# First-layer products of batches 0 and 1 as pairs of 128x64 column halves

## The chip, the cores and the metric

The kernel runs on one core of a Trainium2 chip. The metric is the device time of one execution in microseconds (us); lower is better. Inputs and outputs lie in the chip's memory. One core has a matrix engine (TensorE, PE in the profile, its weight loads listed apart as PEld), VectorE (DVE), ScalarE (ACT), GpSimd (POOL), SyncE (SP), and 16 DMA engines. Sums of products form in PSUM, everything else lies in SBUF.

## The reference, cut to what matters

An attention whose softmax has one more term in the denominator, followed by a two-layer network with a squared ReLU. There are 8 batches, 12 heads, 448 positions, 64 features a head; 3584 tokens, a model width of 768 and a hidden width of 2048.

```python
scale = 1.0 / np.sqrt(q.shape[-1])
scores = scale * np.matmul(q, k.transpose(0, 1, 3, 2))
m = np.max(scores, axis=-1, keepdims=True)
e = np.exp(scores - m)
attn = e / (np.sum(e, axis=-1, keepdims=True) + np.exp(-m) + 1e-09)
x = np.matmul(attn, v)      # then heads side by side: 3584 x 768
...
h = x @ w_in                # 768 x 2048: the first layer
r = np.maximum(h, 0.0)
out = (r * r) @ w_out       # 2048 x 768: the second layer
```

## The kernel before

**Staging.** All eight batches go through the same chain of steps on one core. Scores of a quad of heads (`quad_scores`, tile `sp` in PSUM, products of 64x64 blocks of the array) become exponentials on ACT (`quad_exp`, tiles `et` and `nn`). DVE adds them up (`add_quad`, tile `half`), TensorE sums and multiplies them with v (`sums_of_quad`, `values_step`), ACT forms the reciprocals (`rcp`), and DVE writes the attention's result, transposed, to the batch's tile `xt` (six chunks of 128 features by 448 tokens). Batch 0 is done in two halves of 224 positions at the start (`half_scores` and so on), so that work can begin early.

**The first layer**, which the change touches. For a block of 128 hidden units, `f0`, six products are summed in a PSUM tile `mp`, one for each chunk `dc` of 128 model features: the weights are a 128x128 block of `win`, the moving operand is 448 columns of `xt` (`later_in`, line 513). For a part of batch 0 it is done for two blocks `f0` at once and for 224 columns (`half_in`, line 530), in six pieces of 12 products. All of them go through `product` (line 490), which has two forms. With `cols` false, one matrix product uses the whole 128x128 array. With `cols` true, it is two products of 128 rows by 64 columns, each with half of the weights' columns and the same moving operand; they write partitions 0 to 63 and 64 to 127 of the PSUM tile. In the profile these shapes are 128\*128 and 128\*64. Line 93 is the helper `mm` that records nearly all products, so tiles and shapes tell them apart: `mp<-xt,win` is the first layer, `mp<-wout,gs` the second.

Then ReLU on DVE or ACT (`relu`, tile `rt`), the square on DVE into `gs`, and the second layer in 64x64 blocks (`out_piece`), whose two partial sums DVE adds before the result is stored.

**Who uses which form.** Three stretches of code follow each other. `ORDER` is a list, written out by hand, of steps for the start: batch 0 and most of batches 1 to 3, and in it the first layers of batches 0 and 1 (letters `i` and `j`). `CYCLE` is such a list for a period of two batches; it runs twice, and each run computes 32 first-layer blocks of two earlier batches. The tail computes the first layers of the last two batches (`tile_in`) and the last outputs in order. Before the change the periods alone pass `cols` as true; `ORDER` and the tail leave the default, false:

```python
def later_in(b, f0, c0, c1, cols=False):                             # line 513
"j": lambda n, c0=0, c1=DCH: later_in(*of_tile(n), c0, c1),          # ORDER, line 656
"j": lambda n, c0, c1: later_in(*block(n), c0, c1, True),            # CYCLE, line 741
later_in(b, f0, c, c + 2)                                            # tail, line 783
```

Engines take their instructions in the order of these lists; waits between engines follow from the data. In `ORDER`, the first-layer products stand in blocks between scores, transposes (`transpose_one`, line 207) and values; in the periods they stand in one block.

Of the kernel before, what the change touches and what calls it, by code (L numbers as in the profile page):

```python
# [16 lines left out]
def kernel(  # L17
# [68 lines left out]
    def mp_tile(dtype=FP32):  # L86
        return ring[-1].tile([128, 512 if dtype == FP32 else 1024], dtype, name="mp")
# [4 lines left out]
    def mm(out_, lhsT, rhs, start, stop):  # L92
        return nc.tensor.matmul(out_, lhsT, rhs, start=start, stop=stop)  # L93
# [3 lines left out]
    def load_v_quads(b, g0=0, g1=NQ):  # L97
        if b not in vns:
            vns[b] = v_pool.tile([128, 2, NQ, KC, D], FP16, name="vn")
        vn = vns[b]  # L100
        if b in ON_PE:
            if g1 - g0 == NQ:
                nc.gpsimd.dma_start(out=vn.rearrange("p j g c d -> p (j g) (c d)"), in_=by_pairs["v"][b])
            else:
                nc.gpsimd.dma_start(out=vn[:, :, g0].rearrange("p j c d -> p j (c d)"), in_=by_pairs["v"][b, :, g0::NQ])
            return
        for i in range(2):
            rows_ = vn[64 * i:64 * i + 64].rearrange("p j g c d -> p (j g) (c d)")
            for c0, c1 in ((0, KC - 1), (KC - 1, KC)):
                src = v[:, :, 64 * c0:64 * c1].rearrange("b (hp i) (p t) d -> b i p hp (t d)", i=2, t=c1 - c0)  # L110
                nc.gpsimd.dma_start(out=rows_[:, :, c0 * D:c1 * D], in_=src[b, i])
# [32 lines left out]
    def stage(b):  # L144
        for n, t in (("q", q), ("k", k)):
            st = nc.dram_tensor(f"stage_{n}{b}", (TOTAL,), FP16, kind="Internal").ap()
            stages[n, b] = st
            src = t.rearrange("b h s d -> (b h s d)")
            lo = b * HSD - FRONT
            hi = min(lo + TOTAL, B * HSD)  # L150
            m = (hi - lo) // 1024 * 1024
            for x, y in ((lo, lo + m), (lo + m, hi)):
                if y > x:
                    w = min(y - x, 1024)
                    nc.gpsimd.dma_start(out=st[x - lo:y - lo].rearrange("(r w) -> r w", w=w),
                                        in_=src[x:y].rearrange("(r w) -> r w", w=w), max_dma_last_dim=8192)
            if hi < lo + TOTAL:
                nc.gpsimd.dma_start(out=st[hi - lo:TOTAL].rearrange("(r w) -> r w", r=1),
                                    in_=src[0:lo + TOTAL - hi].rearrange("(r w) -> r w", r=1))
# [3 lines left out]
    def transposed_load(b, i):  # L163
        qk = qk_of(b)
        n, x, c = PLANES[i]
        nc.sync.dma_start(
            out=qk[:, i, 0:c],
            in_=stages[n, b][x:x + c * 2 * D].rearrange("(r c) -> r c", c=2 * D),
            transpose=True,
        )  # L170
# [7 lines left out]
    def tail_keys(b, planes=(1, 2)):  # L178

        if b not in kms:  # L180
            kms[b] = flat.tile([128, H, 64], FP16, name="flatq")
        km = kms[b]
        for which in planes:
            for r in range(2):
                rows_ = slice(64 * r, 64 * r + 64)
                odd, x = (r, 0) if which == 1 else (1 - r, 1 - r)
                src = qks[b][rows_, which, x:x + H * S // 2].rearrange("p (h x) -> p h x", h=H)
                nc.gpsimd.tensor_copy(km[rows_].rearrange("p h (x o) -> p h x o", o=2)[:, :, :, odd],  # L188
                                      src[:, :, S // 2 - 32:S // 2])
# [210 lines left out]
    def quad_scores(m, c):  # L400

        b, g = QUADS[m]
        qk = qks[b]
        if (m, c // 4) not in eqs:
            if g == NQ - 1 and b > 1:
                eqs[m, c // 4] = nat.tile([128, RUN * 2 * S], FP16, name=f"nn{c // 4}")
            else:
                eqs[m, c // 4] = e_pool.tile([128, RUN * 2 * S], FP16, name="et")
        sp = sps["quad", m, c] = s_psum.tile([128, 2, 512], FP32, name="sp")
        if b in ON_PE:  # L410
            for i in range(2):
                for j in range(2):
                    r = slice(64 * j, 64 * j + 64)
                    x = (2 * g + i) * S
                    mm(sp[64 * i:64 * i + 64, j, 0:S], qk[r, 1, x + 64 * c:x + 64 * c + 64],
                       qk[r, 0, x:x + S], start=True, stop=True)
        else:
            n = S // 2
            for j in range(2):
                for i in range(2):  # L420
                    for o in range(2):
                        r = slice(64 * o, 64 * o + 64)
                        h = 2 * NQ * j + 2 * g + i
                        if c == KC - 1:
                            keys = kms[b][r, h, :]
                        else:
                            which, x = (1, h * n + c // 2) if c % 2 == o else (2, h * n + c // 2 + c % 2)
                            keys = qk[r, which, x:x + 190:3]
                        mm(sp[64 * i:64 * i + 64, o, j * n:(j + 1) * n], keys,
                           qk[r, 0, h * n:(h + 1) * n], start=True, stop=True)  # L430

    def quad_exp(m, c):
        exp(chunk_quad(m, c).rearrange("p (o x) -> p o x", o=2), sps.pop(("quad", m, c))[:, :, 0:S])
# [26 lines left out]
    def quad_z(m):  # L460
        zp = zps.pop(m)
        rcp = zqs[m] = z_pool.tile([128, 2, S], FP32, name="rcp")
        nc.scalar.activation(out=rcp, in_=zp[:, :, 0:S], func=AF.Ln, bias=one_b)  # L463
# [23 lines left out]
            nc.vector.tensor_mul(xts[b][:, 2 * g + i, :], xqs[m][i][:, 0:S], zqs[m][:, i, :])  # L487
        del eqs[m, 0], eqs[m, 1], xqs[m], zqs[m]

    def product(out_, lhsT, rhs, start, stop, cols=False):  # L490

        if cols:
            for x in (0, 64):
                mm(out_[x:x + 64], lhsT[:, x:x + 64], rhs, start=start, stop=stop)
        else:
            mm(out_, lhsT, rhs, start=start, stop=stop)
# [13 lines left out]

    hps = {}

    def later_in(b, f0, c0, c1, cols=False):
        if c0 == 0:
            hps[b, "all", f0] = mp_tile()
        hp, xt = hps[b, "all", f0], xts[b]
        for dc in range(c0, c1):
            product(hp[:, 0:S], win[:, dc, f0 * 128:(f0 + 1) * 128], xt[:, dc, :],
                    start=(dc == 0), stop=(dc == DCH - 1), cols=cols)
# [192 lines left out]
    def period(b):  # L712
        m = NQ * (b - 1)
        first = EARLY + 2 * KC * (b - FIRST_PERIOD) // 2

        def following(n):
            ahead, what = ((1, n) if n < 6 else (2, 6) if n < 7 else (1, 6) if n < 8 else (2, n - 8))
            t = b + ahead
            if t < B and (n != 7 or b > FIRST_PERIOD):
                if what < 3:  # L720
                    transposed_load(t, what)
                elif what < 5:
                    tail_keys(t, (what - 2,))
                elif what == 5:
                    load_v_quads(t)
                else:
                    stage(t)

        def block(n):
            return b - 2 + n // NFFB, n % NFFB  # L730

        return {
            "s": lambda x, c: quad_scores(m + x, c),
            "e": lambda x, c: quad_exp(m + x, c),
            "a": lambda x, step: add_quad(m + x, step),
            "S": lambda x: sums_of_quad(m + x),
            "Z": lambda x: quad_z(m + x),
            "M": lambda x: quad_reciprocal(m + x),
            "v": lambda x, c: values_step(m + x, c),
            "X": lambda x: quad_x(m + x),  # L740
            "j": lambda n, c0, c1: later_in(*block(n), c0, c1, True),
            "k": lambda n, act: later_relu(*block(n), act),
            "l": lambda n: later_squared(*block(n)),
            "o": lambda n, f0, f1: out_piece(128 * ((first + n) // 2), HALF * ((first + n) % 2), HALF, range(f0, f1), True),
            "O": lambda n, act: out_first(128 * ((first + n) // 2), HALF * ((first + n) % 2), HALF, act),
            "Q": lambda n: out_second(128 * ((first + n) // 2), HALF * ((first + n) % 2), HALF),
            "d": lambda n: following(n),
        }
# [31 lines left out]

    def tile_in(b, f0):
        for c in range(0, DCH, 2):
            later_in(b, f0, c, c + 2)
        later_relu(b, f0, False)
        later_squared(b, f0)

# [39 lines left out]
```

## Time and profile before

| | |
|---|---|
| median of 3 runs | 392.37 us (391.68 to 394.08) |
| profiled execution | 392.36 us, span from first to last instruction 390.6 us |
| granted TensorE clock | 1.00 in all slices |
| TensorE busy | 381.8 us, 98% of the span, 6432 products |
| DVE, ACT, POOL busy | 65%, 58%, 16% |
| first-layer products | 768 of 128\*64 by 448 columns; 348 of 128\*128 by 448; 72 of 128\*128 by 224 |
| chain that ended last | PE 89%, ACT 5%, the rest 6% |

The busy time counts a stretch in which any product is in flight, and the mean of a product is its latency in the pipeline. As products overlap, the pace of a group must be taken from the starts of its instructions, or from the length of a block in the timeline divided by its products. A line of the timeline gives the start, the length to the end of the last instruction, engine, line, operation, tiles, shape and how many were merged.

### The profile page before, as it was taken

The numbers are of one execution on the slowest core, as the hardware profiler recorded it, in microseconds if no ns is written. First come the engines' busy times: TensorE is split into PE (matmuls) and PEld (weight loads), VectorE is DVE, ScalarE is ACT, GpSimd is POOL, SyncE is SP. The second block draws the span as 40 slices with busy tenths as digits, with TensorE's granted clock in tenths as the row PEclk, the third lists the DMA queues.
The fourth block names the chain that finished last, engine by engine and source line by source line (L and its number), as shares of the span: only waits on it lengthen the run. The fifth ranks groups of instructions, "written<-read, shape, count | busy, mean of one in ns | idle before, by whom it ended". The sixth has DMA issues, their size and how long they took to land.

```text
span 390.6 us, 14257 instructions
## 1 busy us (share of the span) xinstructions
PE 381.8 (98%) x6432; PEld 254.3 (65%) x6432; DVE 253.5 (65%) x468; ACT 228.3 (58%) x308; POOL 61.9 (16%) x96
## 2 busy tenths in 40 slices
PE   9689999999999999999999999999999999999997
PEld 5566656565689865567777665567777755556665
DVE  3887995765765766556968757575878788880000
ACT  5999998586689611249989731248988720001221
POOL 8443420025000700410001240210000000000000
PEclk9999999999999999999999999999999999999999
DMA  8999999999939899903129697901112200001132
GB/s 144 204 204 205 201 199 206 159 203 176 215 84 166 168 186 118 201 2 66 44 59 196 148 178 156 165 4 44 60 48 64 64 23 2 0 0 62 61 82 81
DMA packets 75052, 45.34 MB, mean 116 GB/s; under 512 B 47472, under 2 KB 72944, under 8 KB 74992
## 3 DMA queue, kind: packets, MB, share of 16 engines
q0 software_dynamic: 24752, 22.62, 37.6%
q1 hardware_dynamic: 49952, 21.59, 28.6%
q8 instruction: 50, 0.82, 1.0%
q10 hardware_dynamic: 288, 0.23, 0.2%
q14 instruction: 10, 0.08, 0.1%
HBM read 45.69 MB, written 17.93 MB: 163 GB/s over the span
## 4 chain that ended last, share of the span: by engine, by line
PE 89%; ACT 5%; DMA 2%; DVE 2%; POOL 1%; issue 1%; POOLq 0%; DVEq 0%; ACTq 0%
PE mp L93 79%; PE sp L93 8%; ACT et L254 3%; DMA nn<-in_k_dram 2%; PE mp L207 1%; POOL nn L117 1%; ACT rcp L372 1%; ACT rcp L365 0%; DVE half L441 0%; DVE xt L487 0%; DVE half L443 0%; DVE half L445 0%; ACT rcp L466 0%; ACT rcp L463 0%; DVE half L447 0%
## 5 line engine op out<-in xcount | busy, mean ns | idle before, releaser
L93 PE MATMUL mp<-wout,gs 64*64 64x384 f16 (+2 forms) x2928 | 165.4, 322 | 0.0
L93 PE MATMUL mp<-xt,win 128*64 128x448 f16 (+2 forms) x1188 | 148.3, 347 | 0.1
L93 PEld LDWEIGHTS <-gs 64*64 64x64 f16 (+1 forms) x2928 | 103.8, 106 | 33.9
L93 PEld LDWEIGHTS <-win 128*64 128x64 f16 (+1 forms) x1188 | 83.2, 106 | 63.5 <-issue 4.2
L254 ACT ACTIVATE et<-sp 128x896 f16<-128x896 f32 (+2 forms) x131 | 110.6, 891 | 12.7 <-PE sp L93 12.2
L505 DVE TENSOR_SCALAR rt<-mp 128x448 f16<-128x448 f32 x87 | 54.0, 622 | 15.9 <-PE mp L93 12.9
L509 DVE TENSOR_TENSOR gs<-rt 128x448 f16<-128x448 f16 x128 | 49.4, 404 | 21.9 <-ACT rt L503 20.0
L503 ACT ACTIVATE rt<-mp 128x448 f16<-128x448 f32 x41 | 21.8, 543 | 64.9 <-PE mp L93 50.9
L575 ACT ACTIVATE ot<-mp 128x384 f32<-128x384 f32 (+2 forms) x31 | 14.9, 480 | 70.5 <-PE mp L93 70.4
L93 PE MATMUL sp<-qk 64*64 64x224 f16 (+1 forms) x1056 | 53.3, 274 | 1.9 <-ACT et L254 1.2
L93 PEld LDWEIGHTS <-qk 64*64 64x64 f16 x1056 | 32.8, 114 | 14.3 <-issue 5.7
L188 POOL COPY flatq<-qk 64x384 f16<-64x384 f16 x20 | 14.5, 724 | 169.6 <-DMA qk<-stage_k 169.1
L254 ACT ACTIVATE nn<-sp 128x896 f16<-128x896 f32 x42 | 37.1, 916 | 4.3 <-PE sp L93 4.2
L487 DVE TENSOR_TENSOR xt<-mp,rcp 128x448 f16<-128x448 f32 x42 | 24.3, 620 | 15.6 <-ACT rcp L466 10.0
L581 DVE SCALAR_TENSOR_TENSOR ot<-mp,ot 128x384 f32<-128x384 f32 x42 | 23.4, 557 | 14.0 <-ACT ot L575 11.5
L93 PEld LDWEIGHTS <-vn 64*64 64x64 f16 x756 | 22.5, 107 | 9.8 <-issue 1.4
L93 PE MATMUL mp<-et,vn 64*64 64x448 f16 (+1 forms) x448 | 24.5, 343 | 0.0
L577 DVE TENSOR_SCALAR ot<-mp 128x384 f32<-128x384 f32 x26 | 14.4, 555 | 15.1 <-PE mp L93 14.9
L463 ACT ACTIVATE rcp<-sp,one_b 128x896 f32<-128x896 f32 x21 | 21.1, 1007 | 3.3 <-PE sp L93 3.3
L466 ACT ACTIVATE rcp<-rcp 128x896 f32<-128x896 f32 x21 | 19.9, 949 | 0.5
L441 DVE TENSOR_TENSOR half<-et 128x1792 f16<-128x1792 f16 x15 | 16.5, 1100 | 4.3 <-ACT et L254 4.2
L443 DVE TENSOR_TENSOR half<-half,et 128x1792 f16<-128x1792 f16 x15 | 16.3, 1087 | 0.3
(59 smaller groups left out, 195.7 us busy)
## 6 DMA issues: line engine op xcount, KB each, us to landing
out_dram<-ot SPq DMA_DIRECT2D x52, 96.0 KB, 2.4
out_dram<-ot SPq DMA_DIRECT2D x19, 192.0 KB, 1.9
win<-in_moe_w_in_dram POOLq DMA_DIRECT2D x8, 384.0 KB, 12.3
wout<-in_moe_w_out_dram POOLq DMA_DIRECT2D x4, 768.0 KB, 15.3
vn<-in_v_dram POOLq DMA_DIRECT2D x10, 288.0 KB, 7.9
stage_q<-in_q_dram POOLq DMA_DIRECT2D x4, 676.0 KB, 14.0
stage_k<-in_k_dram POOLq DMA_DIRECT2D x4, 676.0 KB, 16.7
nn<-in_q_dram POOLq DMA_DIRECT2D x8, 224.0 KB, 8.9
```

Source lines behind the costliest of these rows:

```text
L93: return nc.tensor.matmul(out_, lhsT, rhs, start=start, stop=stop)
L254: nc.scalar.activation(out=out_, in_=in_, func=AF.Exp, scale=scale)
L441: nc.vector.tensor_add(esq[m], a[:, 0:w], a[:, w:2 * w])
L443: nc.vector.tensor_add(esq[m], esq[m], z[:, 0:w])
L463: nc.scalar.activation(out=rcp, in_=zp[:, :, 0:S], func=AF.Ln, bias=one_b)
L466: nc.scalar.activation(out=zqs[m], in_=zqs[m], func=AF.Exp, scale=-1.0)
L487: nc.vector.tensor_mul(xts[b][:, 2 * g + i, :], xqs[m][i][:, 0:S], zqs[m][:, i, :])
L503: nc.scalar.activation(out=rt[:, 0:m], in_=hp[:, 0:m], func=AF.Relu)
L505: nc.vector.tensor_scalar(out=rt[:, 0:m], in0=hp[:, 0:m], scalar1=0.0, scalar2=None, op0=ALU.max)
L509: nc.vector.tensor_mul(gs[:, f0:f0 + per, t0 % RING:t0 % RING + n], r, r)
L575: nc.scalar.activation(out=ot, in_=op[:, 0:w], func=AF.Copy, scale=OUT_SCALE)
L581: nc.vector.scalar_tensor_tensor(out=ot, in0=lo[:, 0:w], scalar=OUT_SCALE, in1=ot, op0=ALU.mult, op1=ALU.add)
```

## The change

`product` and `later_in` get true as default for `cols`. The periods no longer pass it, and the tail passes false. So `half_in` and the `j` steps of `ORDER`, which pass nothing, change from one form to the other: 72 products of 224 columns and 156 of 448 become 144 and 312 products of 128\*64. Periods and tail compute as before.

```diff
-    def product(out_, lhsT, rhs, start, stop, cols=False):
+    def product(out_, lhsT, rhs, start, stop, cols=True):
...
-    def later_in(b, f0, c0, c1, cols=False):
+    def later_in(b, f0, c0, c1, cols=True):
...
-            "j": lambda n, c0, c1: later_in(*block(n), c0, c1, True),
+            "j": lambda n, c0, c1: later_in(*block(n), c0, c1),
...
     def tile_in(b, f0):
         for c in range(0, DCH, 2):
-            later_in(b, f0, c, c + 2)
+            later_in(b, f0, c, c + 2, False)
```

## The prediction

> **What bounds the kernel now.** I read the page's busy times first, then the chain that ended last, then TensorE's own timeline around the products that change, and last the groups kept apart by shape. TensorE is busy for 98% of the span and carries 89% of the chain, 79% of it in the tile mp, which the products of both layers write. So whatever the change does to TensorE's pace shows in the time, except where the chain runs elsewhere. That is so only at the start and in one gap:
>
> ```profile
> span 390.6 us, 14257 instructions
> PE 381.8 (98%) x6432; PEld 254.3 (65%) x6432; DVE 253.5 (65%) x468; ACT 228.3 (58%) x308; POOL 61.9 (16%) x96
> PE 89%; ACT 5%; DMA 2%; DVE 2%; POOL 1%; issue 1%; POOLq 0%; DVEq 0%; ACTq 0%
> ```
>
> In the chain in order of time, ACT's exponentials and reciprocals set the path from 17.3 to 33.0 us. From 33.0 on TensorE does, but for 79.6 to 88.8 us (ACT and DVE, a chain that itself starts from a score tile of TensorE), so a delay before it is passed on whole:
>
> ```profile
> 30.82 2.13 ACT et L254 x3
> 32.99 0.38 PE sp L93 x4
> 33.37 2.39 PE mp L93 x12
> ...
> 72.30 6.92 PE mp L93 x36
> 79.22 0.34 PE sp L93 x4
> 79.58 0.92 ACT et L254
> ...
> 92.96 8.05 PE mp L93 x42
> ```
>
> The products to compare, by shape: 768 half-array products (128x64 weights, 448 columns) are those of the periods; of the 348 full-array ones of 448 columns 156 belong to batches 0 and 1 and change, 192 belong to the tail and stay; the 72 of 224 columns (batch 0 by halves of its sequence) all change. PEld gives the weight loads.
>
> ```profile
> L93 PE MATMUL mp<-xt,win 128*64 128x448 f16 x768 | 73.0, 353 | 0.0
> L93 PE MATMUL mp<-xt,win 128*128 128x448 f16 x348 | 67.9, 353 | 0.0
> L93 PE MATMUL mp<-xt,win 128*128 128x224 f16 x72 | 7.9, 259 | 0.1
> L93 PEld LDWEIGHTS <-win 128*64 128x64 f16 x768 | 43.3, 110 | 29.1 <-issue 0.3
> L93 PEld LDWEIGHTS <-win 128*128 128x128 f16 x420 | 39.8, 98 | 34.4 <-issue 3.9 <-DVE rt L505 0.3
> ```
>
> The mean of one (353 ns in both shapes) is a latency; products overlap. The pace is in the starts of whole blocks, which the timeline merges:
>
> ```profile
> 42.75 1.75 PE L207 MATMUL mp<-ident,nn 128*64 128x128 f16 x56
> 44.43 0.38 PE L93 MATMUL sp<-qk 64*64 64x448 f16 x4
> ...
> 71.75 0.55 PE L93 MATMUL sp<-qk 64*64 64x448 f16 x8
> 72.23 6.98 PE L93 MATMUL mp<-xt,win 128*128 128x448 f16 x36
> 79.15 0.38 PE L93 MATMUL sp<-qk 64*64 64x448 f16 x4
> ...
> 134.47 0.58 PE L93 MATMUL sp<-qk 64*64 64x224 f16 x16
> 134.99 36.51 PE L93 MATMUL mp<-xt,win 128*64 128x448 f16 x384
> 171.43 0.59 PE L93 MATMUL sp<-qk 64*64 64x224 f16 x16
> ```
>
> **The change, part by part.** The compiled order of TensorE holds 228 products more and 228 weight loads more (72 of 224 columns become 144, 156 of 448 become 312); the order on DVE, ACT, POOL and SP is the same up to buffer numbers, and so are the waits on the changed products. The tail's products keep the whole array. No DMA is added or moved.
>
> *Steady pace, 448 columns.* Full: 36 products last 6.98 us, the last of them 0.353, so 35 steps take 6.63 and one takes 189.4 ns. Pairs: (36.51 - 0.35) / 191 steps = 189.3 ns a pair; read one by one, the second of a pair starts 2 to 4 ns after the first. 156 x (189.3 - 189.4) is 0.0 us.
>
> *Steady pace, 224 columns.* Full products start every 96 ns (25.42, 25.51, 25.61 us and so on). A 224-column pair is not in the trace. Bound below: the 64x64 products of 224 columns, which start every 96 ns in groups of four. Bound above: each half-load takes 110 ns by its record; if the two loads of a pair ran one after the other, a pair would take 220 ns, 124 more. The nearest row is the transposes: 128x64 weights with 128 columns, 56 in 1.75 us; (1.75 - 0.22) / 27.5 is 56 ns a pair, so two half-loads fit into 56 ns, less than 96. I take 0. Of the 72, 36 lie before 33 us, under ACT's path, and 36 on the path (blocks at 36.4, 46.1 and 58.8 us); the upper bound is thus 36 x 124 = 4.5 us.
>
> [...]
>
> *Changes of shape at the ends of blocks.* The changed products stand in 14 blocks, 11 of them after 33 us, and each has 64x64 work on both sides, as before. Into a full block from 448-column scores the step is 282 ns where the stream is 189: 93 ns lost. Out of one it is 283: again 93. Pairs and transposes lose the same: out of the period's block 283 ns, into one from 224-column scores 186 against 96 (90 lost), into transposes 279 and out of them 149 against 56 (93). So I carry over -3 ns at the entry. In a full block the second product starts 200 ns after the first (10 above the pace), in the period's block the second pair starts 213 ns after (23 above): +13. The last half starts 3 ns after its partner: +3. Sum 13 a block, 11 x 13 = +0.1 us. Bounds: 90 ns of one change more for each block (11 x 0.09 = +1.0 us) or both changes saved (11 x 2 x 0.093 = -2.0 us).
>
> *Fetching 456 more instructions and reading xt twice.* In the period the same four instructions per 189 ns run without a step above 213 ns, and the 64x64 work around the changed blocks issues faster yet, so I cost both at nothing: the 189 ns of each step cover them. If they did not, each step of a changed block would lengthen, which is rival 3. The DMA load is alike in the two places:
>
> ```profile
> 33.00:80.00 47.00, 46.87 (x618) 26.84 (x621) 34.80 (x65) 38.67 (x52) 9.20 (x13) 1.00 1.25 196
> 139.80:158.70 18.90, 18.90 (x204) 11.32 (x202) 12.59 (x28) 3.14 (x7) 2.16 (x4) 1.00 1.21 153
> ```
>
> (The last three numbers are granted clock, DMA share and GB/s.)
>
> *Sum.* The profiled execution took 392.36 us around its span of 390.6, next to the median of 392.37. 392.36 + 0.0 + 0.0 + 0.1 gives 392.5 us.
>
> **Rivals.**
> 1. *The 64-wide columns stay as they are between pairs and 64x64 work, so no drain.* Both shapes use half the columns, the full one all of them, so the change of shape might be cheaper. Both changes saved at 11 blocks: -2.0 us, 390.4. Against it stand the 186 and 283 ns at the ends of the period's block, which is this very neighbourhood. Chance 0.05.
> 2. *Half-loads queue and bound the 224-column pairs* (the other side: slower). Place: the three blocks on the path; it decides once a pair of loads takes over 96 ns. At 220 ns it costs 4.5 us: 396.9, slower by 1.2%; halfway between the transposes' 56 and 220, at 138 ns, 36 x 42 = 1.5 us: 394.0. For it: such a pair isn't in the trace, and half-loads are the slower ones by record. Against: 56 ns a pair in the transposes. Chance 0.03 for the full price, 0.04 for the half one. [...]
> 3. *Some pairs don't run side by side* in these short blocks, where products with waits stand close. One that runs serially costs its pace again: all on the path, 156 x 0.189 + 36 x 0.096 = 33 us, 425; one in eight gives 396.6. Against: among the period's pairs 64 products carry a wait, and no step is above 213 ns. Chance 0.03.
> That the edit touches nothing is excluded: the compiled order has the 228 more products.
>
> **How the numbers follow.** Forecast (the pace and the block ends stay): 0.85, 392.5 us. Rival 1: 0.05. Rival 2: 0.04 at the half price, 0.03 at the full one. Rival 3: 0.03. A difference under 1%, 3.9 us, is about what a measurement here can't tell from none. Forecast, rival 1 and the half price lie within it, 0.94; I move 0.01 of it to faster, because rival 1 would also shorten three blocks before 33 us, which I priced at nothing. Slower has the full price and rival 3, 0.06. The range goes from rival 1's 390.4 to the upper bound of the block ends, 392.4 + 1.0 = 393.4, with the spread of the runs above their median (394.08 - 392.37 = 1.7): 395.1. The half price lies in it, too.
>
> **What would show it right or wrong.** In the profile after: groups of half-array products x1080 of 448 columns and x144 of 224, full ones x192; the blocks at 72 and 93 us still last 6.9 and 8.0 us; the 224-column blocks last 1.2 us for 24 products; gaps to the neighbouring scores stay near 283 ns; the granted clock stays 1.00. Rival 1 would show 190 ns there, rival 2 a longer 224-column block alone, rival 3 steps of 380 ns within blocks. If the time moves by over 1% while the block lengths stay, the reasoning from TensorE's pace is wrong as a whole.

## The result and the profile after

The changed kernel takes 393.56 us (median; before 392.25 us in the same series): the ratio is 1.0033, interval 1.0023 to 1.0043. That is 1.3 us more, clear of noise, and under the 1% that the prediction counted as a difference. The forecast was 392.5 us, range 390.4 to 395.1.

The page of the changed kernel:

```profile
span 392.5 us, 14712 instructions
PE 384.5 (98%) x6660; PEld 259.7 (66%) x6660; DVE 253.3 (65%) x468; ACT 228.7 (58%) x308; POOL 63.7 (16%) x96
PEclk9889999999999999999999999999999999999999
q8 instruction: 52, 0.85, 0.9%
PE 90%; ACT 2%; DMA 2%; DVE 2%; POOL 1%; issue 1%; POOLq 0%; DVEq 0%; ACTq 0%
```

Two readings. First, ACT's share of the chain went from 5% to 2%: the stretch of the start that ACT bounded has become TensorE's (after_again, the second profile, has 2% as well). Second, this one execution was granted half a clock from 16.0 to 22.8 us (0.52 in the mean of 16 to 23 us), ahead of the first changed product (the two 8s of the clock row), so its lag of 2.0 us at 24 us is not the change. The second profile, after_again, is of the same kernel and has the full clock throughout; I compare with that one.

The groups by shape and the block of 36 products (now 72 halves) in the timeline of the first profile:

```profile
L93 PE MATMUL mp<-xt,win 128*64 128x448 f16 x1080 | 104.6, 353 | 0.0
L93 PE MATMUL mp<-xt,win 128*128 128x448 f16 x192 | 36.5, 353 | 0.0
L93 PE MATMUL mp<-xt,win 128*64 128x224 f16 x144 | 8.0, 260 | 0.1
...
74.39 7.00 PE L93 MATMUL mp<-xt,win 128*64 128x448 f16 x72
81.33 0.38 PE L93 MATMUL sp<-qk 64*64 64x448 f16 x4
```

7.00 us stands against 6.98 for the same work as full products. From first to last start a changed block grew by some 17 ns, whatever its length: 6648 against 6631 ns (36 full products), 3243 against 3226 (18), 1082 against 1065 (12 of 224 columns); one, at 38.41 us, grew by 31. Each is entered 3 ns sooner (279 ns in place of 282). Eleven such blocks on the path make 0.2 us. Where is the rest of the 1.3 us? In the timeline of after_again, TensorE stands still at 33 us, in the middle of a group of eight score products:

```profile
32.17 0.38 PE L93 MATMUL sp<-qk 64*64 64x448 f16 x4
32.38 0.84 PE L93 MATMUL xp<-et,vn 64*64 64x224 f16 x28
33.05 0.27 PE L93 MATMUL xp<-half,ones 64*64 64x224 f16 x4
33.15 0.35 PE L93 MATMUL sp<-qk 64*64 64x448 f16 x1
34.63 0.57 PE L93 MATMUL sp<-qk 64*64 64x448 f16 x7 [1.13 <-issue]
```

One product runs, and the seven others come 1.48 us later. "issue" says that the profile shows nothing that they waited for, no semaphore either. In the kernel before, the same eight ran as one piece: four, a step of 0.41 us, which the wait for ACT's exponential ends, four more.

```profile
32.47 0.27 PE L93 MATMUL xp<-half,ones 64*64 64x224 f16 x4
32.57 0.81 PE L93 MATMUL sp<-qk 64*64 64x448 f16 x8
33.31 2.44 PE L93 MATMUL mp<-xt,win 128*128 128x448 f16 x12
```

1.48 - 0.41 leaves 1.07 us. The chain of after_again has it, too, as a piece of its own:

```profile
33.32 0.18 PE sp L93
33.50 1.13 issue
34.63 0.57 PE sp L93 x7
```

### The profile page after: what moved, and what is told of

Its sections match the earlier page's. It is cut to its first block, busy times and chain, and to the rows that moved or that the text cites. A ratio compares the mean times of both kernels' runs of the same rounds, so it can differ in the third digit from the quotient of the medians.

```text
span 392.5 us, 14712 instructions
## 1 busy us (share of the span) xinstructions
PE 384.5 (98%) x6660; PEld 259.7 (66%) x6660; DVE 253.3 (65%) x468; ACT 228.7 (58%) x308; POOL 63.7 (16%) x96
## 4 chain that ended last, share of the span: by engine, by line
PE 90%; ACT 2%; DMA 2%; DVE 2%; POOL 1%; issue 1%; POOLq 0%; DVEq 0%; ACTq 0%
PE mp L93 80%; PE sp L93 9%; DMA nn<-in_k_dram 2%; PE mp L207 1%; ACT et L254 1%; POOL nn L117 1%; PE xp L93 0%; DVE xt L487 0%; ACT rcp L372 0%; DVE half L441 0%; DVE half L443 0%; ACT rcp L466 0%; ACT rcp L463 0%; DVE half L445 0%; POOL vn L105 0%
## 5 line engine op out<-in xcount | busy, mean ns | idle before, releaser
L93 PEld LDWEIGHTS <-win 128*64 128x64 f16 (+1 forms) x1416 | 85.8, 108 | 61.3 <-issue 4.2
L188 POOL COPY flatq<-qk 64x384 f16<-64x384 f16 x20 | 16.3, 816 | 170.3 <-DMA qk<-stage_k 137.9
L581 DVE SCALAR_TENSOR_TENSOR ot<-mp,ot 128x384 f32<-128x384 f32 x42 | 23.4, 557 | 13.7 <-ACT ot L575 11.1
L93 PEld LDWEIGHTS <-vn 64*64 64x64 f16 x756 | 23.7, 111 | 10.2 <-issue 1.7
```

The source lines that it names most:

```text
L581: nc.vector.scalar_tensor_tensor(out=ot, in0=lo[:, 0:w], scalar=OUT_SCALE, in1=ot, op0=ALU.mult, op1=ALU.add)
```

## What stops TensorE: its instructions

Queue q8, kind "instruction", moved 50 packets before and 52 after, 16,384 bytes each. Of the kernel before:

```profile
q8 instruction: 50, 0.82, 1.0%
```

TensorE has 12,864 products and weight loads before and 13,320 after; divided by 256 that is 50.3 and 52.0. So q8 feeds TensorE, 256 instructions a packet. I counted the products and loads in the compiled order and put the counts beside the starts in the trace. The steps without a semaphore come at one place, instruction 190 of 256 (702, 958, 1214, within two products). That is the limit between two blocks of 256, and TensorE enters a block when it starts the block's first instruction. Theory F, formed here, and a guess in its first half: entering a block of 256 is what lets the fetch of the next one start, and where TensorE uses up a block faster than the next one comes, it stands still. For the block that begins with instruction 1214, from the starts of the packets and of the products in the traces (us; the last column is the time from 958 to 1214):

| kernel | enters 958 | packet starts | enters 1214 | packet to 1214 | block took |
|---|---|---|---|---|---|
| before | 28.83 | 31.82 | 37.34 | 5.5 | 8.5 |
| after_again | 28.54 | 32.14 | 34.63 | 2.5 | 6.1 |
| half_only | 27.88 | 31.43 | 33.72 | 2.3 | 5.8 |
| early_pairs | 28.78 | 32.30 | 34.62 | 2.3 | 5.8 |
| early_split | 28.01 | 31.34 | 33.78 | 2.4 | 5.8 |
| late_pairs | 27.87 | 31.06 | 34.95 | 3.9 | 7.1 |

In the four kernels that stand still, the packet starts 3.3 to 3.6 us after the entry and the first instruction runs 2.3 to 2.5 us after the packet's start: some 6.0 us for 256 instructions, 43 a microsecond. The kernel before needs 8.5 us for the 256 ahead of 1214 and never feels the limit there. With the three blocks of batch 0's first half in pairs, 72 instructions are added, and TensorE would be done with it sooner than the next can come.

What sets off a fetch is the part of F that these traces do not show. The packet for the block from 1214 starts 2.3 us after the entry of 958 in the first profile of the changed kernel (30.04 to 32.37 us) and 4.2 us after it in lean, a kernel below (29.17 to 33.41); in tail_pairs, also below, one starts 1.2 us ahead of the entry that should have let it start (46.69 against 47.89 us, block 1470). What all profiles share is that up to 35 us the packets start at least 5.9 us apart and that a block's first instruction runs 2.2 us or more after its packet's start. That shows how fast the blocks come; what lets a fetch start stays open.

## The experiments

The time between two marks, the third group of sums of batch 0 (`xp<-half,ones`, at 24.25 us in the kernel before) and the first sums of batch 1 (`sp<-half,ones`, at 47.33 us), is free of what happens ahead of 24 us. It is in the last column, from one profile each; from the second mark to the start of the last product all of them need 340.0 to 340.3 us.

| kernel | ratio to before, interval | median us | marks, us |
|---|---|---|---|
| before | 1 | 392.2 | 23.1 |
| changed, again (after_again) | 1.0032, 1.0018 to 1.0045 | 393.45 | 24.5 |
| 224-column products only (half_only) | 1.0052, 1.0032 to 1.0072 | 394.34 | 24.4 |
| 448-column products only (later_only) | 1.0013, 1.0001 to 1.0026 | 392.46 | 23.4 |
| tail in pairs (tail_pairs) | 1.0003, 0.9991 to 1.0016 | 392.28 | 23.1 |
| three early blocks in pairs (early_pairs) | 1.0034, 1.0021 to 1.0047 | 393.42 | 24.7 |
| all but those three (late_pairs) | 1.0002, 0.9994 to 1.001 | 392.27 | 23.2 |
| three early blocks cut by columns (early_split) | 1.0035, 1.0023 to 1.0048 | 393.28 | 24.1 |
| before without 16 helpers (lean) | 1.001, 0.9999 to 1.0021 | 392.36 | 23.1 |
| changed without 16 helpers (after_lean) | 1.0026, 1.0007 to 1.0045 | 393.22 | 24.4 |

**Which part.** First the changed kernel again, with no edit (A, B and C were the theories before F was formed):

> The changed kernel once more, for a second profile. Theory A (block ends): each of the 11 changed blocks on the path is 17 ns longer, as the first profile has it (3243 against 3226 ns for 18 full products, 6648 against 6631 for 36), so the loss is 0.2 us and what is above that in the times (1.3 us) sits at the start, where the granted clock fell to half in the first profile: lag of the first changed product 0 to 2 us and varying. Theory B (start): the lag is over 1 us ahead of or within the half-sequence blocks of batch 0 (24 to 33 us), at a full clock too. Theory C (clock): this kernel draws a half clock in the start more often than the one before. Time 393.0 to 394.0 us by all of them.

It gave the second profile: full clock, first changed product only 0.5 us later than before, loss of 1.4 us between the marks. C falls: none of these 11 runs has a mean clock under 0.999, of the first 22 only the profiled one (0.991), and the medians agree. B stands, and A covers 0.2 us. Then two halves of the change:

```diff
 half_only, against the changed kernel
-        "j": lambda n, c0=0, c1=DCH: later_in(*of_tile(n), c0, c1),
+        "j": lambda n, c0=0, c1=DCH: later_in(*of_tile(n), c0, c1, False),
 later_only, against the changed kernel, in half_in
-                        start=(dc == 0 and jf == 0), stop=(dc == DCH - 1 and jf == 1))
+                        start=(dc == 0 and jf == 0), stop=(dc == DCH - 1 and jf == 1), cols=False)
```

> Only the 72 products of 224 columns of batch 0 become pairs; the 156 of 448 columns stay whole. Theory A: 0.05 us slower than the kernel before (3 blocks on the path). Theory B: the whole 1.0 to 1.3 us is here, 393.4 us, since these products lie in the stage that ACT's chain bounds. A theory that it is the number of instructions of the program gives about a third of it, 0.4 us.

> Only the 156 products of 448 columns become pairs; the 72 of 224 columns stay whole. Theory A: 0.15 us slower than the kernel before. Theory B: no loss, 392.3 us. The number of instructions as cause: two thirds of it, 0.9 us slower, 393.1.

The step at 33 us is in half_only (1.21 us) and not in later_only, so it belongs to the 224-column products. The 0.3 us between the marks of later_only are more than block ends: three blocks hold products of both widths, and where only one width is in pairs they change shape inside, for some 0.12 us each (1458 against 1336 ns and 2323 against 2200 between the marks, 1945 against 1821 behind them). The changed kernel has no such change inside a block. In half_only the same blocks take 1474, 2320 and 1943 ns, which explains 0.3 of the 0.9 us by which its median lies above that of after_again; the rest stays open, and the intervals overlap. The size of the program as such:

```diff
 tail_pairs, against the kernel before, in tile_in
-            later_in(b, f0, c, c + 2)
+            later_in(b, f0, c, c + 2, True)
```

> Batches 0 and 1 as before; the tail's 192 products of the whole array become 384 of 128x64 instead: the program grows by 384 instructions, at the other end. Theories A and B: no change at the start, 0.0 to 0.1 us, 392.3 us, as there are no changes of shape in the tail except one at its beginning and one ahead of the last outputs. The size of the program as cause: about 1.1 us slower, 393.4.

384 more instructions cost nothing there that the runs resolve (ratio 1.0003). It is not their number in the program.

**Which blocks, and shape or count.** With F at hand, the three blocks before 33 us alone, then all the others, then the three blocks with as many instructions but in full-array shape:

```diff
 early_pairs, against the kernel before, in half_in (cols=(half == 0)); late_pairs, against the changed one (cols=(half == 1))
-                        start=(dc == 0 and jf == 0), stop=(dc == DCH - 1 and jf == 1))
+                        start=(dc == 0 and jf == 0), stop=(dc == DCH - 1 and jf == 1), cols=(half == 0))
 early_split, against the kernel before, in half_in
-                product(hp[:, jf * FIRST:(jf + 1) * FIRST], win[:, dc, f:f + 128], xt[:, dc, x0:x0 + FIRST],
-                        start=(dc == 0 and jf == 0), stop=(dc == DCH - 1 and jf == 1))
+                w = FIRST // 2 if half == 0 else FIRST
+                for y in range(0, FIRST, w):
+                    product(hp[:, jf * FIRST + y:jf * FIRST + y + w], win[:, dc, f:f + 128], xt[:, dc, x0 + y:x0 + y + w],
+                            start=(dc == 0 and jf == 0 and y == 0), stop=(dc == DCH - 1 and jf == 1 and y + w == FIRST))
```

> Only the three blocks of the first half of batch 0 (36 products of 224 columns, before 33 us) become pairs. Theory F (fetch of instructions): TensorE's instructions come in blocks of 256; entering one asks for the next, which lands some 6.0 us later while the DMA engines are full; 36 products and 36 loads more let TensorE reach instruction 1214 before its block has landed, and it stands still in the middle of a group of scores at 33 us without a semaphore to wait for. So the whole loss of about 1.1 us is here: 393.3 us, with a step of 1.2 to 1.5 us at instruction 1212. Theory A (block ends): these blocks lie under ACT's path, no loss: 392.2 us.

> The change without those three blocks: all other products of batches 0 and 1 are pairs. Theory F: no still stand at 33 us; only the block ends remain, 11 x 17 ns = 0.2 us: 392.4 us. If the half-array shape of the 224-column products costs time as such, half of the loss of the changed kernel stays: 392.9 us.

> The kernel before with the same three blocks cut the other way: each product of the whole array by 224 columns becomes two of the whole array by 112 columns. As many instructions as with pairs, but no half-array product in the start. Theory F: the same loss as with the three blocks in pairs, about 1.1 us, 393.3 us, and the same step without a wait near instruction 1212. If the shape is the cause: 392.2 us.

All three came as F has it: 1.2 us, nothing, 1.1 us. In early_pairs the limit before it, at 28.2 us, costs a step of 0.6 us, too, which lengthens its marks to 24.7. The 192 products left in late_pairs (156 and 36) as pairs cost nothing that these runs resolve. In late_pairs the eight scores run as one piece, as in the kernel before:

```profile
31.61 0.81 PE L93 MATMUL sp<-qk 64*64 64x448 f16 x8
```

In early_split no first-layer product before 35 us is a half-array one, and TensorE stands still at the same instruction; its timeline:

```profile
31.30 0.36 PE L93 MATMUL mp<-xt,win 128*128 128x112 f16 x4
31.59 0.38 PE L93 MATMUL sp<-qk 64*64 64x448 f16 x4
31.80 0.84 PE L93 MATMUL xp<-et,vn 64*64 64x224 f16 x28
32.48 0.27 PE L93 MATMUL xp<-half,ones 64*64 64x224 f16 x4
32.57 0.35 PE L93 MATMUL sp<-qk 64*64 64x448 f16 x1
33.78 0.57 PE L93 MATMUL sp<-qk 64*64 64x448 f16 x7 [0.86 <-issue]
```

The shape is out as a cause; the count in that place is it.

**Moving the limit.** Both kernels without 16 helper products on constants in the first transposes and scores, 32 instructions fewer ahead of all this (the diff for both):

```diff
         x, n = 64 - 64 * j, 128 * (c1 - c0)
-        mm(aside()[x:x + 64, 0, 0:n], idle[:, x:x + 64], idle[:, 0:n], start=True, stop=True)
...
-            for z in (0, 64):
-                mm(aside()[z:z + 64, j, 0:n], idle[y, z:z + 64], idle[y, 0:n], start=True, stop=True)
```

> The kernel before without its 16 helper products on constants in the first transposes and first scores (32 instructions fewer ahead of instruction 260; their output is read by nobody). Theory F: the limits of the blocks move by 32 instructions against the work; the small still stand at instruction 702 (0.2 to 0.7 us in the profiles with batches 0 and 1 as before) is eased: 391.7 to 392.2 us. A theory in which these products keep the granted clock up: slower by 1 us or more, with a half clock before 25 us.

> The changed kernel with all its pairs, but without the 16 helper products on constants at the start (32 instructions fewer ahead of instruction 260; by themselves they moved the kernel before by 0.2 us, the profiled span not at all). Theory F: what counts is where the limit of a block of 256 instructions falls. It moves from instruction 1214 of the changed kernel to what was instruction 1246 there, in the pairs that follow the scores; TensorE enters the block before at some 28.5 us, so the next one lands at 34.5, about when TensorE needs it. No still stand at 33 us: 392.4 to 392.7 us. A theory by which the mere number of instructions in the first 35 us costs the time leaves nearly all of the loss: 393.3 us.

Neither did what I expected. In lean the step at instruction 702 is gone, and the time is not better: right behind it TensorE waits for a semaphore (0.6 to 1.3 us at instruction 706 in the profiles), which took in the step all along. Three of the twelve runs of lean have a mean clock of 0.996 and take 393.4 to 393.8 us, and none of the 23 runs of the kernel before in that series has; whether these products bear on the clock is not settled. In after_lean the loss stayed at 1.0 us. The limit did move: TensorE runs through the group of scores, and the step stands in the pairs behind it, again at a limit of 256 (instruction 1210 of this program):

```profile
33.22 0.38 PE L93 MATMUL sp<-qk 64*64 64x448 f16 x4
33.53 0.95 PE L93 MATMUL mp<-xt,win 128*64 128x448 f16 x8
34.86 1.71 PE L93 MATMUL mp<-xt,win 128*64 128x448 f16 x16 [0.38 <-issue]
```

It is half as large, 734 ns where 189 are the pace, but the limit before it, at 28.1 us, now costs a step, too (642 ns where 86 is the usual one). Above the pace these are 0.55 and 0.56 us, together the 1.1 us of the one step. What I had missed is that a stretch of 12 us with little slack in it pays at each limit, so moving the limits by 32 instructions only shares the loss out. It confirms where the steps come, and my arithmetic for its size failed.

**The fetch by itself.** The last second-layer products cut into eight by columns, where the DMA engines have a share of 0.24 in the kernel before (1.24 between 24 and 34 us):

```diff
 tail_split, against the kernel before, in out_piece
-                mm(op[:, 0:w], g, wout[:, fb, n0:n0 + w], start=(fb == 0), stop=(fb == NFFB - 1))
+                s = w // 8
+                for y in range(0, w, s):
+                    mm(op[:, y:y + s], g, wout[:, fb, n0 + y:n0 + y + s],
+                       start=(fb == 0 and y == 0), stop=(fb == NFFB - 1 and y + s == w))
```

> The kernel before with each of the 240 last second-layer products of the whole array cut into eight by columns (48, 32 or 16 columns each): some 80 instructions a us where the DMA engines are at a fifth of their load at the start (share 0.24 against 1.24). It measures the fetch by itself, and is slower for sure. If a block of 256 instructions always takes 6 us to come, TensorE stands still once in 256 instructions, every 16 of the old products, until 6 us are full: 15 blocks x 6 us = 90 us for the last stage in place of 36. If the 6 us are owed to the load of the DMA engines, the blocks come in 3 to 4 us and the stage goes on at the pace of the products, 16 x 8 x 25 to 30 ns = 3.2 to 3.8 us a block, 50 to 60 us for the stage.

This kernel takes 410.39 us (before 392.08, one run of each), its last stage 54 us, within the second of the two forecasts; the share in that stage is 0.20. Products start every 25 ns, 3.2 us for 128, and every 128 products, thirteen times in a row, there is a step of 0.24 to 1.08 us. The weight loads around the first two of them:

```profile
356.92 2.07 PEld L93 LDWEIGHTS <-gs 128*128 128x128 f16 x79
359.20 3.31 PEld L93 LDWEIGHTS <-gs 128*128 128x128 f16 x128 [0.21 <-issue]
362.93 8.14 PEld L93 LDWEIGHTS <-gs 128*128 128x128 f16 x302 [0.42 <-issue]
```

From step to step it is 3.45 to 4.29 us, so a block of 256 comes in that time here and in 6.0 at the start. The parts differ as follows: entry to the packet's start 1.0 to 1.9 us here, 3.3 to 3.6 there; from the packet's start to the first instruction 2.2 to 2.6 us here, 2.3 to 2.5 there. So the time lies ahead of the packet. A busier set of DMA engines would fit that, but their share alone does not: in after_again it is 1.24 again from 123.65 to 131.99 us, and there the packets start 3.94 and 4.39 us apart, against 5.89 and 6.08 from 20.2 to 32.1 us at 1.25. By the packets in the trace, queue q0 (software_dynamic) makes up that load at the start and queue q1 (hardware_dynamic) the later one. Which transfers fill the engines may thus be what counts; no run here changes them in the start, so the reason for the 6.0 us stays open.

No kernel of these is faster than the one before.

## Why the prediction was right or wrong

The forecast of no difference above 1% held, and 393.56 lies in the range; the sum predicted +0.1 us where 1.3 was measured. The range holds by luck as far as the mechanism goes: its upper end is made of 1.0 us for block ends and 1.7 for the spread of the runs, with nothing for the instructions. And the prediction took a difference under 1% for one that can't be told from none; 22 runs of each kernel told 0.33%. By its steps:

- *Steady pace.* Right for both widths: 72 halves last 7.00 us against 6.98, and 24 halves of 224 columns grew by 17 ns a block, so a pair goes at the pace of a full product. Rival 2, queueing half-loads, is refuted: the pairs of 224 columns go at 96 ns, where its half price needed 138.
- *Block ends.* 13 ns a block were predicted, and 14 were measured (17 longer from first to last start, 3 less at the entry); the steps at the changes of shape stayed (279 in, 283 out). Rival 1, with both changes of shape saved, did not happen.
- *Fetching 456 more instructions: nothing.* This is the step that failed. I compared with the period's rate, 21 instructions a microsecond at a similar DMA share, and with the 64x64 work around the blocks. I looked for long steps and never asked how much slack there was. At the start the kernel before uses them up at 30 to 35 a microsecond (256 in 8.5 and in 7.2 us for the blocks from 958 and from 702), next to the limit of 43. The cover that I named, the 189 ns of each step, does not apply to the 224-column products at all, which start every 96 ns.
- *36 products under ACT's path: nothing.* Wrong for the same reason. Those products hide behind ACT, but their instructions don't: they pushed TensorE to a limit of 256 too soon, in the scores that ACT waits for next. That is 1.1 of the 1.3 us.
- *Rival 3* had steps without a cause within blocks, from products that don't run side by side; what came is a step in the scores behind them, with another cause.

## What to carry to other kernels

TensorE's instructions came at a rate of their own here: 256 in some 6.0 us in the start, 43 a microsecond, and 256 in 3.45 to 4.29 us in the tail of tail_split. Before splitting products at equal pace, count TensorE's instructions in each stretch of 256, and compare the time of the stretch with what a block took to come there; here two blocks of the start had 1.2 and 2.5 us of slack, and 72 instructions used them up. In a trace, a product that stands apart within a group, with "issue" as what ended the idle time and at a multiple of 256 from the last such place, was the sign of it here (702, 958, 1214). The total of instructions said little: 384 more in the tail had a ratio of 1.0003.

## What was new about the hardware here

A block of 256 instructions took 5.8 to 6.1 us to come in the start, at a DMA share of 1.24, and 3.45 to 4.29 us in the tail, at 0.20; the share alone is not the measure, as packets came 3.9 and 4.4 us apart at 1.24 later on. At limit 1214 in the four kernels that stood still there, and at the limits of tail_split, TensorE had no more than the next block under way: that block's packet started 3.3 to 3.6 us after the entry of the block before, and 1.0 to 1.9 us in the tail. And the half clock was granted inside the first 25 us of an execution whose program there is unchanged (16.0 to 22.8 us in the first profile); that execution lost 2.0 us before the first changed product and had no step at the scores, as the rest of the start came late enough for its instructions: 1214 ran at 34.58 us, 2.2 us after its packet's start.
